# Seven block products for a third of K in h · w_out of a fused float64 attention and MLP kernel

## The chip, the cores and the metric

The kernel runs on one core of a Trainium2 chip. The metric is device time in microseconds (us) of the slowest core (here the only one); lower is better. Times of the kernel before and of the changed one are medians of several runs; the profile is one more execution, with a time of its own.

## The reference, cut to what matters

Three blocks follow one another. Window attention gives 2304 tokens of 512 columns, `x`. Then two gated networks, all in matrix products:

```python
g, val = x @ w_gate, x @ w_val            # 512 -> 1536
h = g * sigmoid(g) * val                  # 2304 x 1536
x2 = h @ w_out                            # 1536 -> 512, the product that the change touches
a, b = x2 @ w1, x2 @ w2                   # 512 -> 1024
out = ((a * b) @ w3) @ w_out2             # done as (a * b) @ (w3 @ w_out2)
```

## The kernel before, in words

**Words and passes.** Weights arrive as 64-bit numbers and are narrowed to 32 bits by VectorE (DVE) and ScalarE (ACT). Each 32-bit operand is split into two words, a high one (a `cast`, on ACT) and what is left (a `rest`, on DVE). A product of two blocks is three passes over the words: high x high, high x low, low x high (`PASSES`). A matmul works on 128 x 128 weights and 384 token columns (`T`).

**The stages.** First the attention (to about 113 us). The second stage (`gated`, to 363 us) computes h; the third (`project`, to 513 us) computes x2; the fourth (`gated` again, to 688 us) computes a * b; then `final` multiplies w3 by w_out2 and the result by that. Tokens are worked in three groups of 768 (`tp`), each as two halves of 384.

**Seven products in `gated`.** A unit is one pair of 128-column blocks of one weight for one token group. Its 2 x 2 block product is done with seven products of six matmuls (numbers 1 to 7, list `PRODUCTS`) instead of eight. Product 1 goes into a PSUM bank `al`; ACT copies it (negated) out into a tile `c11`; product 2 goes into a bank `ga` of its own, and DVE adds it to `c11` (L699). Products 6, 7 and 4 add onto `al`, with a copy by ACT (L377) after each of the first two; products 5 and 3 share a bank `be`. ACT then applies the Silu (L712) or DVE multiplies the two halves of the gate (L709). `AT` says in which slot of the order a product stands; a unit starts every seven slots, so that two units interleave. The finished h goes to DRAM (`store`, L777).

**The third stage in `project`, plain.** For each token group eight banks `acc[m, x]` collect 12 row blocks `f` of w_out's K: in each, 4 column blocks m, 2 token halves x, 3 passes, so 24 matmuls (L852), 288 in a group. Row tiles of h (`Rows`: 128 x 768, two row blocks, one token half) come from DRAM (`pl`, on SP's queue), get their high word on ACT (`ph`, L218) and their rest on DVE (L227). 16 tiles of w_out's words stay resident through all three groups. At a group's end ACT (L835, and the negated ones L377) and DVE (L838) evict the eight banks into `X2`. `Operands` then makes the fourth stage's operands from it: 14 casts, 14 rests and 8 sums for each group.

**w_out's words.** `Split.make` narrows a 256-row piece of w_out, splits it in two steps of 512 columns (L218, L227) and stores it to DRAM, from where `Resident.queue` loads it. It is interleaved with the gate weights in the list `coming`, through two staging buffers (`st`), so that a load waits until the piece two before it is made.

**What sets the order.** All engines' instructions are put in line by hand under `manual_schedule`. `Plan` keeps a model clock for each engine; small work (splits, loads, DMAs) is queued as a `Job` with a cost, a rank and a due time, and `fill` places what is ready between the products. `need` places a job at once when a product asks for it. `slots` counts free tiles of the pool `sl`. Each engine, and each DMA queue (SP's, and POOL's for adding DMAs), then works strictly in the order in which it was given its instructions. `events1` and `events_p` tie queueing of loads to units and row blocks. Lines named by the trace: L687 a product's matmul in `gated`, L852 in `project`, L377 a copy by ACT, L699 an add by DVE, L811 the load of a row tile, L263 the load of a staging buffer.

## Time and profile before

| what | us |
|---|---|
| runs: median (lowest to highest), 3 runs | 823.98 (823.34 to 825.07) |
| the profiled execution, its own time | 825.91 |
| its span, first to last instruction | 824.2 |
| PE busy in the span | 815.6 |
| third stage, `project` | 150.0 |

PE is TensorE's matmuls, PEld its weight loads, SPq and POOLq the DMA queues of SyncE and GpSimd. Times in rows are us from the span's start unless they say ns. In a row of groups the name `out<-in` is what is written and read, with buffer numbers left out, `x` and a number is how many instructions, then busy us, mean ns of one, and the idle time before them with what ended it. Matmuls are pipelined, so a matmul lasts 334 ns while the next starts 173 ns after it.

### The profile page before, as it was taken

How to read it: one execution, taken by the hardware profiler on the slowest of the kernel's cores; microseconds unless marked ns; L12 is line 12 of the kernel's file. 1: busy time of each engine (PE TensorE's matmuls, PEld its weight loads, DVE VectorE, ACT ScalarE, POOL GpSimd, SP SyncE). 2: the span in 40 equal slices, each digit the busy share in tenths (PEclk: the TensorE clock that was granted, in tenths of full speed). 3: DMA queues.
4: the chain of work that ended last, by engine and by line, in shares of the span. 5: the costliest groups of instructions: out<-in, count | busy, mean ns of one | idle time of the engine just before them, and what ended most of it. 6: DMA issues, size and time to landing. Idle time of an engine off the chain costs nothing.

```text
span 824.2 us, 15599 instructions
## 1 busy us (share of the span) xinstructions
PE 815.6 (99%) x5718; PEld 785.2 (95%) x5718; DVE 640.6 (78%) x1354; ACT 454.6 (55%) x1194; POOL 92.4 (11%) x135
## 2 busy tenths in 40 slices
PE   9999999999999999999999999999999999999998
PEld 6777899999999999999999999999999998899997
DVE  5999889686887939865888683877888844789994
ACT  7899987555555535633564551444444423755543
POOL 3666833000000000000000000000010100000000
PEclk9999999999999999999999999999999999999999
DMA  9989396253562344599996722024555289007632
GB/s 187 199 186 199 61 217 125 90 192 128 192 229 83 137 153 161 210 360 380 385 290 157 233 71 103 20 83 142 167 180 175 110 299 335 27 2 207 181 73 78
DMA packets 172766, 140.23 MB, mean 170 GB/s; under 512 B 120849, under 2 KB 142609, under 8 KB 171665
## 3 DMA queue, kind: packets, MB, share of 16 engines
q1 hardware_dynamic: 167888, 125.86, 50.8%
q0 software_dynamic: 4800, 13.37, 5.9%
q8 instruction: 45, 0.74, 0.4%
...
## 4 chain that ended last, share of the span: by engine, by line
PE 90%; SPq 4%; DMA 2%; ACT 1%; DVE 1%; issue 1%; ACTq 0%
PE o L852 18%; PE ala L687 15%; PE alb L687 14%; PE bea L687 7%; PE beb L687 7%; PE acc L1010 5%; PE al L1153 4%; PE gaa L687 4%; PE gab L687 3%; SPq L403 2%; PE be L1153 2%; PE al L1085 2%; PE PV L519 2%; PE PT L499 2%; PE S L466 1%; PE T L429 1%
## 5 line engine op out<-in xcount | busy, mean ns | idle before, releaser
L852 PE MATMUL o<-ph,wo 128*128 128x384 f32 x576 | 146.4, 334 | 0.0
L852 PEld LDWEIGHTS o<-ph,wo 128*128 128x128 f32 x576 | 104.1, 188 | 0.0
L852 PE MATMUL o<-pl,wo 128*128 128x384 f32 x288 | 96.3, 334 | 0.0
L377 ACT ACTIVATE ha<-ala 128x384 f32<-128x384 f32 x102 | 49.6, 488 | 50.0 <-PE ala L687 49.3
L777 POOL DMA_DIRECT2D h<-ha x24 | 13.0, 546 | 548.2 <-DVE ha L709 548.2
L699 DVE TENSOR_TENSOR ha<-ha,bea 128x384 f32<-128x384 f32 x60 | 33.2, 553 | 38.3 <-PE bea L687 22.3
L852 PEld LDWEIGHTS o<-pl,wo 128*128 128x128 f32 x288 | 54.1, 188 | 0.3 <-DVE pl L227 0.3
L480 ACT ACTIVATE pexp<-S,stat 128x128 f32<-128x128 f32 x144 | 53.1, 421 | 0.0
L218 ACT CAST hf<-h 128x384 fp32r<-128x384 f32 x84 | 38.8, 513 | 14.5 <-DVE h L231 13.2
L712 ACT ACTIVATE ha<-ha 128x384 f32<-128x384 f32 x54 | 28.4, 526 | 33.1 <-DVE ha L699 33.1
L227 DVE TENSOR_TENSOR hf<-h,hf 128x384 fp32r<-128x384 f32 x84 | 42.3, 548 | 4.8 <-ACT hf L218 4.8
L227 DVE TENSOR_TENSOR pl<-pl,ph 128x768 fp32r<-128x768 f32 x36 | 33.4, 953 | 14.6 <-ACT ph L218 14.3
L218 ACT CAST ph<-pl 128x768 fp32r<-128x768 f32 x36 | 29.1, 839 | 26.2 <-DMA pl<-h 23.6
L490 POOL TENSOR_TENSOR pexp<-pexp,stat 128x384 f32<-128x384 f32 x48 | 39.1, 835 | 28.6 <-DVE stat L487 14.1
L377 ACT ACTIVATE c12b<-alb 128x384 f32<-128x384 f32 x30 | 14.8, 492 | 48.7 <-PE alb L687 48.6
L480 ACT ACTIVATION_READ_ACCUMULATOR pexp<-S,stat 128x1 f32 x144 | 37.2, 260 | 0.0
L699 DVE TENSOR_TENSOR c22b<-c22b,beb 128x384 f32<-128x384 f32 x30 | 16.6, 553 | 25.8 <-ACT c22b L377 25.8
L687 PE MATMUL ala<-xo,w_g_7h 128*128 128x384 f32 x120 | 30.4, 336 | 0.5 <-ACT ha L377 0.5
L687 PE MATMUL ala<-xo,w_g_1h 128*128 128x384 f32 x126 | 29.2, 335 | 0.0
L473 DVE TENSOR_REDUCE stat<-S 128x3 f32<-128x384 f32 x48 | 24.4, 550 | 4.8 <-PE S L466 4.4
L218 ACT CAST xp<-X 128x384 fp32r<-128x384 f32 x42 | 19.7, 520 | 10.5 <-DVE X L231 7.5
L377 ACT ACTIVATE c11b<-alb 128x384 f32<-128x384 f32 x30 | 14.7, 490 | 19.2 <-PE alb L687 19.2
...
## 6 DMA issues: line engine op xcount, KB each, us to landing
...
```

Of the source, the lines that this page charges most:

```text
L218: (eng.copy if eng is nc.scalar else eng.tensor_copy)(out=hi(), in_=src())
L227: return plan.job(lambda eng: eng.tensor_tensor(out=lo(), in0=src(), in1=hi().bitcast(F32), op=ALU.subtract), after, slots=slots, due=due, ...
L377: nc.scalar.mul(out=out, in_=in_, mul=-1.0)
L473: nc.vector.tensor_reduce(out=st[:, 0, x, :], in_=sc[2 * m + x], op=ALU.max, axis=AX.X, negate=True)
L480: nc.scalar.activation(out=pe[:, jj, :], in_=so[:, jj, :], func=AF.Exp, bias=st[:, 0, x, jj:jj + 1], accum_out=st[:, 1, x, jj:jj + 1])
L490: nc.gpsimd.tensor_tensor(out=pe, in0=pe, in1=st[:, 3, x, :].unsqueeze(2).to_broadcast([P, SUB, P]), op=ALU.mult)
L687: nc.tensor.matmul(acc, lhsT=self.wt.ops[p, x][:, m, :], rhs=self.xs.ops[p, m][:, y, :], start=start and n == 0, stop=n == 5, skip_group_c ...
L699: nc.vector.tensor_tensor(out=out, in0=x, in1=y, op=ALU.add)
L712: nc.scalar.activation(out=h, in_=src, func=func, scale=-1.0 if direct else 1.0)
L852: nc.tensor.matmul(acc[m, x], lhsT=wos.tiles[i // 6][:, i % 6, :], rhs=rows[2 * tp + x].words(f, b), start=f == n == 0, stop=f == NF - 1 a ...
L1010: nc.tensor.matmul(acc, lhsT=w3T[i][c // 3][:, x, (c % 3) * P:(c % 3) * P + P], rhs=zt[c, y], start=c == k == 0, stop=c == NI - 1 and k == 2)
L1153: nc.tensor.matmul(acc, lhsT=right.ops[p, m, y][:, P * k:P * k + P], rhs=self.xs.ops[p, m][:, x, :], start=bool(name) and n == 0, stop=n = ...
```

## The change

It does the first two of the six 256-row pairs of w_out's K (`SEVEN`) as seven products per token group, the other four (`plain`) block by block as before. In `project` product 1 goes into a bank `al`, ACT copies it into a second bank (`seed`), and product 2 and later the plain blocks are added there by TensorE; product 7 seeds a fourth bank in the same way. The sums of h's blocks that the seven products need are made in DRAM: the second stage writes h's blocks of the first two pairs several times (`spread`), with the sign of the diagonal ones turned in the last multiplication, and POOL's queue issues four adding DMAs for each token group as soon as the second pair is stored. A new class `Seven` makes w_out's words for the seven products, with four sums for each piece. Units from number 6 on, counted from 0 (`SEEDED`), in both `gated` stages use the same seeding for product 2 and do product 5 ahead of it (`AT_SEEDED`). w_out's words are queued directly behind the weight ahead of them in the list, with a due time, and at the weights' rank. Row tiles have a budget of their own (8 loaded, 6 high words) and are loaded strictly in turn; resident tiles of w_out become 20. The last pair's units stand in another order (`ENDS`). The fourth stage's operands of the first two token groups wait for a mark that the third group's second step sets (`opened`).

```diff
 AT = {1: 0, 2: 2, 5: 3, 6: 4, 7: 8, 4: 12, 3: 13}
...
+AT_SEEDED = {1: 0, 5: 2, 2: 3, 6: 4, 7: 8, 4: 12, 3: 13}
...
-    NSLOT = 56
+    NSLOT = 58
...
-    half = ctx.enter_context(tc.tile_pool(name="half", bufs=7))
+    half = ctx.enter_context(tc.tile_pool(name="half", bufs=5))
...
+            if j.large:
+                j.done = self.landed = max(j.done, self.landed + 2.6)
+            if j.rows:
+                self.rows[j.rows] -= 1
...
-                        if j.slots and self.slots < j.slots + self.keep:
+                        if j.slots and self.slots < j.slots + self.keep or j.rows and (self.rows[j.rows] < 1 or j.behind and j.behind.done is None):
...
+    SEEDED = 6
+    SEVEN = (0, 1)
+    stored = {}
...
-                if self.x and direct:
+                if self.x and (direct or i == t and func != AF.Copy and self.fp in SEVEN):
                     nc.vector.scalar_tensor_tensor(out=h, in0=src, scalar=-1.0, in1=h, op0=ALU.mult, op1=ALU.mult)
                     plan.charge("DVE", dve(T))
...
+                elif (i, t) == (0, 0) and self.seeded:
+                    nc.scalar.copy(out=h, in_=src)
+                    plan.charge("ACT", act(T))
...
-                    self.c11 = self.own(0, 0, "c11")
+                    self.seeded = self.n >= SEEDED
+                    if self.seeded:
+                        self.ga = bank(f"ga{self.name}")[:, :T]
+                    self.c11 = self.ga if self.seeded else self.own(0, 0, "c11")
                     later(1, lambda: self.copy(self.c11, self.al))
+                elif p == 2 and self.seeded:
+                    plan.wait(self.read)
+                    self.mm(self.ga, 2)
+                    self.put(0, 0, self.ga)
                 elif p == 2:
-                    ga = bank(f"ga{self.name}")[:, :T]
-                    self.mm(ga, 2, True)
-                    self.add(self.c11, self.c11, ga)
+                    self.ga = bank(f"ga{self.name}")[:, :T]
+                    self.mm(self.ga, 2, True)
+                    self.add(self.c11, self.c11, self.ga)
...
-                        for i, t in enumerate(hs.pop((self.fp, self.tp))):
-                            store(out=hd[self.fp, self.tp][:, i, :], in_=t)
-                        plan.slots += 2
+                        h = hs.pop((self.fp, self.tp))
+                        if func != AF.Copy and self.fp in SEVEN:
+                            spread(self.fp, self.tp, h)
+                        else:
+                            for i, t in enumerate(h):
+                                store(out=hd[self.fp, self.tp][:, i, :], in_=t)
+                            plan.slots += 2
+                            done = mark()
+                            done.done = plan.charge("DVE", 0.0) + 4.0
+                            stored[self.fp, self.tp] = [done]
...
-        when = [(7 * n + AT[p], n, p) for n in range(len(units)) for p in PRODUCTS if (n, p) != (len(units) - 1, 2)]
+        when = [(7 * n + (AT_SEEDED if n >= SEEDED else AT)[p], n, p) for n in range(len(units)) for p in PRODUCTS if (n, p) != (len(units) - 1, 2)]
...
+    H_AT = {1: 0, 7: 1, 2: 2, 3: 3, 4: 4, 6: 5, 5: 6}
+    def spread(fp, tp, h):
+        to, f = h7d[tp], SEVEN.index(fp)
+        (h0, h1) = (t.rearrange("p (c t) -> p c t", c=2) for t in h)
+        for at, src in (((0, 2), h0), ((2, 4), h1), ((4, 6), h1), ((6, 7), h0[:, :1])):
+            nc.sync.dma_start(out=to[:, at[0]:at[1], f, :], in_=src)
+        plan.slots += 2
+        if fp == SEVEN[1]:
+            keep, plan.rank = plan.rank, SPREAD_RANK
+            done = mark()
+            done.done = plan.charge("DVE", 0.0) + 5.0
+            def add(p, by, after):
+                j = plan.job(lambda eng: eng.dma_start(out=to[:, H_AT[p]], in_=to[:, H_AT[by]], accum_op=ALU.add),
+                             [done, *after], lag=8.0, DMA=1.0)
+                stored[p, tp, 7] = [j]
+                return j
+            s5 = add(5, 7, [])
+            add(7, 3, [s5])
+            s6 = add(6, 5, [s5])
+            add(4, 6, [s6])
+            for p in (1, 2, 3):
+                stored[p, tp, 7] = [done]
+            plan.rank = keep
...
+        before = None, None
+        def __init__(self, tp):
+            self.tp = tp
...
+                eng.dma_start(out=self.lo[key].bitcast(F32),
+                              in_=h7d[self.tp][:, H_AT[f]] if x == 7 else h1d[f, self.tp][:, :, T * x:T * x + T])
...
+            a = loading(load, stored[key[0], self.tp, 7] if key[1] == 7 else stored[key[0], self.tp], rows=1, lag=9.0, due=due)
+            b = cast(hi, lambda: self.lo[key].bitcast(F32), [a], 2 * T, 0, rows=2, due=due)
+            (a.behind, b.behind), Rows.before = Rows.before, (a, b)
+            self.jobs[key] = rest(lambda: self.lo[key], lambda: self.lo[key].bitcast(F32), lambda: self.hi[key], [b], 2 * T, due=due)
+        def words(self, key, g, x):
+            return (self.lo if x else self.hi)[key][:, g, :]
+    STEPS = (1, 5, 6, 2, 7, 3, 4)
...
-            acc = {(m, x): bank(f"o{tp}_{m}_{x}")[:, :T] for m in range(NM) for x in range(2)}
...
-            for f in range(NF):
...
-                            plan.need(wos.jobs[i // 6])
-                            nc.tensor.matmul(acc[m, x], lhsT=wos.tiles[i // 6][:, i % 6, :],
-                                             rhs=rows[2 * tp + x].words(f, b),
-                                             start=f == n == 0, stop=f == NF - 1 and n == 2)
...
-            if tp == NTP - 1:
-                for m, x in acc:
-                    evict(m, x)
-            xop2[tp] = Operands([lambda x=x: x for x in x2], f"xp{tp}")
...
+            al, ga, be, de = ([None] * 2 for _ in range(4))
...
+            def seed(to, src, m, name):
+                open_bank(to, m, name)
+                nc.scalar.copy(out=to[m], in_=src[m])
+                plan.charge("ACT", act(T))
...
+            def copy(r, c, src, m):
+                (negated if r == c else nc.scalar.copy)(out=part(r, c, m), in_=src[m])
+                plan.charge("ACT", act(T))
+            def add(r, c, src, op, m):
+                nc.vector.tensor_tensor(out=part(r, c, m), in0=part(r, c, m), in1=src[m], op=op)
+                plan.charge("DVE", dve(T))
+            def product(acc, key, w, g, m, start=False, stop=False):
+                plan.need(r.jobs[key])
+                for n, (x, y) in enumerate(PASSES):
+                    plan.need(wos.job(w, g, x, m))
+                    nc.tensor.matmul(acc, lhsT=wos.words(w, g, x, m), rhs=r.words(key, g, y),
+                                     start=start and n == 0, stop=stop and n == 2, skip_group_check=not start)
...
+            for k, p in enumerate(STEPS):
+                for event in events.get((tp, k), ()):
                     event()
...
+                to = {2: ga, 5: be, 3: be}.get(p, al)
+                for m in range(2):
+                    if p in (1, 5):
+                        open_bank(to, m, "al" if p == 1 else "be")
+                    for g in range(2):
+                        product(to[m], (p, 7), p, g, m, p in (1, 5) and g == 0, True)
+                    if p == 1:
+                        seed(ga, al, m, "ga")
+                    elif p == 5:
+                        copy(1, 1, be, m)
+                    elif p == 6:
+                        copy(0, 1, al, m)
+                    elif p == 7:
+                        seed(de, al, m, "de")
+                    if m:
+                        freed(1)
+                        if tp == NTP - 1:
+                            wos.used(k)
+                    plan.advance(PRODUCT)
+                    yield
+            for k, fp in enumerate(plain):
+                for event in events.get((tp, len(STEPS) + k), ()):
+                    event()
+                for g in range(2):
+                    last = g == 1 and fp == plain[-1]
+                    for b, (i, c, to) in enumerate(((1, 0, al), (0, 1, be), (0, 0, ga), (1, 1, de))):
+                        for m in range(2):
+                            product(to[m], (fp, c), (fp, i), g, m, False, last)
+                            if last:
+                                if (i, c) == (1, 0):
+                                    copy(1, 0, al, m)
+                                elif (i, c) == (0, 1):
+                                    add(0, 1, be, ALU.add, m)
+                                elif (i, c) == (0, 0):
+                                    copy(0, 0, ga, m)
+                                else:
+                                    add(1, 1, de, ALU.subtract, m)
+                        if b == 1 or b == 3:
+                            if b == 3 and g:
+                                freed(2)
+                                if tp == NTP - 1:
+                                    wos.used(len(STEPS) + 2 * k)
+                                    wos.used(len(STEPS) + 2 * k + 1)
+                            plan.advance(2 * PRODUCT)
+                            yield
+            xop2[tp] = Operands([lambda x=x: x for x in x2], f"xp{tp}", dict.fromkeys(PRODUCTS, opened), X2_SUMS, X2_RESTS, due=14.0 * tp)
...
+    class Seven(Doubles):
+        GROUPS = ((1, 2), (5, 6), (7, 3), (4,))
...
+                for q, p in enumerate(group):
+                    after, due = list(ready), self.due + k + q
+                    if p in sums:
+                        x, y, op = sums[p]
+                        after = after + [made.get({6: 5, 3: 6}.get(p))]
...
+                        made[p], after = j, [j]
...
+                    a = cast(hi, lambda p=p: self.words(*at[p]), after + by[-2:-1], n, 0, p == 1, due=due)
+                    b = rest(lambda p=p: ops[p][:, 1], lambda p=p: self.words(*at[p]), lambda p=p: ops[p][:, 0], [a], n, 0, p == 1, due)
+                    self.last += [a, b]
+                    jobs.append(b)
+                def put(eng, group=group, t=t):
+                    for q, p in enumerate(group):
+                        eng.dma_start(out=w7d[p][:, SEVEN.index(self.n)], in_=t[0][:, q].rearrange("p x f -> p (x f)").bitcast(F32))
+                by.append(plan.job(put, jobs, lag=5.0, SP=0.5 * len(group)))
+                for p in group:
+                    self.stored[p] = by[-1]
...
+    h7d = [dram.tile([P, 7, 2, T], F32, name=f"h7_{tp}") for tp in range(NTP)]
+    w7d = {p: dram.tile([P, 2, 512], F32, name=f"w7_{p}") for p in STEPS}
...
-    wo = [Split(w_out, n, "wo", put_wo) for n in range(NF2)]
+    wo = [Seven(w_out, n) if n in SEVEN else Split(w_out, n, "wo", put_wo) for n in range(NF2)]
...
-            plan.rank = rank if rank is not None else 1 if isinstance(coming[at[1]], Weights) else 2
+            plan.rank = rank if rank is not None else 2 if coming[at[1]] in w3s else 1
...
             plan.rank = 0
+        if at[1] < len(coming) and (coming[at[1]] in wo or isinstance(coming[at[1]], Plain)):
+            coming[at[1]].due = coming[at[1] - 1].due + 7.0
+            make_to(coming[at[1]], rank, ahead)
...
-    passed = {(tp, f): mark() for tp in range(NTP) for f in range(DF // P)}
...
+        def queue(self, k, due):
+            for s in range(4 * k // 3, -(-4 * (k + 1) // 3)):
+                if s in self.jobs:
+                    continue
+                parts = sorted({768 * s // 1024, (768 * s + 767) // 1024})
...
+                after = []
+                for q in parts:
+                    f, x = self.sources[q]
+                    after += [wo[fp].stored[f] for fp in SEVEN] if x == 7 else [wo[f // 2].stored[f % 2]]
+                self.jobs[s] = plan.job(load, after, lag=7.0, slots=1, due=due, SP=0.5 * len(parts))
...
+    def project_loads(tp):
...
+        for k, p in enumerate(STEPS):
+            rows[tp].queue((p, 7), 100 * tp + k)
+        for k, fp in enumerate([fp for fp in range(NF2) if fp not in SEVEN]):
             for x in range(2):
...
+                rows[tp].queue((fp, x), 100 * tp + len(STEPS) + 2 * k + x)
...
-    order1 = unit_order(NF2, [(x, tp) for x in range(2) for tp in range(NTP)])
-    order2 = unit_order(NI2, [(0, 0), (0, 1), (1, 0), (1, 1), (0, 2), (1, 2)])
+    ENDS = [(0, 0), (0, 1), (1, 0), (1, 1), (0, 2), (1, 2)]
+    order1, order2 = unit_order(NF2, ENDS), unit_order(NI2, ENDS)
...
-    on(events1, last1 - 2, lambda: make_to(wo[-1]))
-    on(events1, last1 - 1, lambda: project_loads(0, range(1)))
-    on(events1, last1, lambda: project_loads(0, range(1, NF2)))
+    ROWS = (8, 6)
+    def share():
+        plan.slots -= sum(ROWS)
+        plan.rows[1:] = ROWS
+    on(events1, last1 - 2, lambda: (make_to(wo[-1]), weight_loads(0, 4)))
+    on(events1, last1 - 1, lambda: (share(), project_loads(0), weight_loads(4, 7)))
+    on(events1, last1, lambda: weight_loads(7, 9))
     events_p = {}
-    on(events_p, (0, 0), lambda: (setattr(plan, "landing", 10.0), make_to(w3s[NW3 - 1])))
+    on(events_p, (0, 0), lambda: (setattr(plan, "landing", 10.0), setattr(plan, "keep", 0), make_to(w3s[NW3 - 1])))
+    for n in range(3):
+        on(events_p, (0, 2 * n), lambda n=n: weight_loads(9 + 2 * n, 11 + 2 * n))
+    on(events_p, (0, 7), lambda: project_loads(1))
+    on(events_p, (1, 7), lambda: project_loads(2))
+    opened = mark()
+    X2_SUMS, X2_RESTS = (), ()
+    SPREAD_RANK = 0
+    on(events_p, (1, 4), lambda: make_to(left2[0, 1], 0))
+    on(events_p, (2, 1), lambda: reach(opened))
     on(events_p, (2, 0), lambda: setattr(plan, "landing", 6.0))
-    on(events_p, (1, 6), lambda: make_to(left2[0, 1], 0))
-    on(events_p, (0, 6), lambda: project_loads(1, range(NF2)))
-    on(events_p, (1, 6), lambda: project_loads(2, range(NF2)))
...
+        plan.slots += sum(ROWS)
+        plan.keep = 3
+        on(events2, 6, lambda: setattr(plan, "keep", 2))
```

## Rows read from the trace of the kernel before

**Rows 1.** The page, busy time of each engine (part 1).
```profile
PE 815.6 (99%) x5718; PEld 785.2 (95%) x5718; DVE 640.6 (78%) x1354; ACT 454.6 (55%) x1194; POOL 92.4 (11%) x135
```

**Rows 2.** The chain that ended last: start us, us, what.
```profile
363.35 149.99 PE o L852 x864
```

**Rows 3.** Waits of PE, whole span: us in total, times, longest us.
```profile
PE alb L687 <- ACT c22b L377: 0.8, 1, 0.8
PE ala L687 <- ACT ha L377: 0.5, 1, 0.5
```

**Rows 4.** Windows: us, then PE, PEld, DVE, ACT, POOL busy (instructions), PEclk, DMA share, GB/s.
```profile
113.65:363.35 249.70, 248.90 (x1431) 248.03 (x1432) 195.56 (x411) 140.42 (x310) 10.13 (x12) 1.00 0.51 168
363.35:378.00 14.65, 14.65 (x87) 14.65 (x86) 11.07 (x19) 6.51 (x9) 0.00 (x0) 1.00 1.04 379
378.00:413.35 35.35, 35.35 (x205) 35.08 (x204) 23.07 (x36) 16.09 (x25) 0.00 (x0) 1.00 1.02 385
413.35:513.35 100.00, 100.00 (x578) 100.00 (x578) 72.45 (x134) 46.01 (x86) 0.00 (x0) 1.00 0.57 171
513.35:530.00 16.65, 16.65 (x98) 16.65 (x97) 12.42 (x27) 8.86 (x20) 0.00 (x0) 1.00 0.00 1
530.00:688.07 158.07, 158.07 (x913) 158.07 (x913) 120.25 (x252) 67.72 (x150) 11.92 (x22) 1.00 0.54 168
```

**Rows 5.** Groups by line, DVE and ACT in the third stage (363.35 to 513.35).
```profile
L227 DVE TENSOR_TENSOR pl<-pl,ph 128x768 fp32r<-128x768 f32 x34 | 31.6, 953 | 14.6 <-ACT ph L218 14.3
L227 DVE TENSOR_TENSOR xp<-X,xp 128x384 fp32r<-128x384 f32 x28 | 14.4, 549 | 0.0
L838 DVE TENSOR_SCALAR X<-o 128x384 f32<-128x384 f32 x8 | 4.5, 558 | 19.0 <-PE o L852 19.0
L218 ACT CAST ph<-pl 128x768 fp32r<-128x768 f32 x34 | 27.6, 840 | 26.2 <-DMA pl<-h 23.6 <-PE o L852 2.3
L835 ACT COPY X<-o 128x384 f32<-128x384 f32 x8 | 3.8, 491 | 22.4 <-PE o L852 22.4
```

**Rows 6.** Groups by line, DVE and ACT in the second stage (113.65 to 363.35).
```profile
L699 DVE TENSOR_TENSOR c11b<-c11b,gab 128x384 f32<-128x384 f32 x17 | 9.3, 547 | 0.0
L227 DVE TENSOR_TENSOR by_wo<-st_wo,by_wo 128x512 fp32r<-128x512 f32 x12 | 8.1, 690 | 2.8 <-ACT by_wo L218 2.4
L231 DVE TENSOR_TENSOR st_v<-st_v 128x256 f32<-128x256 f32 x20 | 7.8, 419 | 0.0
L377 ACT ACTIVATE c11b<-alb 128x384 f32<-128x384 f32 x17 | 8.3, 487 | 4.3 <-PE alb L687 4.3
L218 ACT CAST by_wo<-st_wo 128x512 fp32r<-128x512 f32 x12 | 7.7, 654 | 0.0
L218 ACT CAST w_v_1h<-st_v 128x256 fp32r<-128x256 f32 x11 | 4.2, 412 | 0.0
```

**Rows 7.** Timeline, 298.83 to 311.54: start us, us, engine, what, [idle before].
```profile
298.83 0.43 SPq L263 DMA_DIRECT2D st_g<-in_moe_w_gate_dram  x1
308.31 0.77 DVE L194 TENSOR_SCALAR st_g<-st_g 128x512 int32<-128x512 int32 x2 [2.77 <-DMA st_g<-in_moe_w_gate_dram]
308.69 0.33 PE L687 MATMUL alb<-xo,w_v_1l 128*128 128x384 f32 x1
311.54 0.49 ACT L377 ACTIVATE c11b<-alb 128x384 f32<-128x384 f32 x1
```

**Rows 8.** Waits of ACT in the third stage.
```profile
ACT ph L218 <- DMA pl<-h: 23.6, 10, 6.6
```

**Rows 9.** The tile pl: its loads, and who waited for them.
```profile
  DVE pl L227: 0.3, 1
DMA to landing us min/median/max: 3.5/6.1/9.2
```

**Rows 10.** DMA issues: KB each, median us to landing.
```profile
X<-X POOLq DMA_DIRECT2D x10, 192.0 KB, 5.5
```

156 lines of the change are left out of this document (84 added, 72 removed).

## The prediction

> **What bounds the kernel now.** I read the page's busy times first, for the engine with the least room: TensorE (PE) is busy for 815.6 of 824.2 us, VectorE (DVE) for 78%, ScalarE (ACT) for 55% [rows 1]. Then the chain that ended last, to see whether the stage that the change cuts lies on it: the whole third stage, h times w_out, is one piece of 149.99 us with 864 matmuls and nothing in between [rows 2]. That is 149.99 / 864 = 0.1736 us a matmul, and 6 x 0.1736 = 1.04 us for a product of six. So a matmul less in this stage shortens the program, as long as nothing else becomes late. Then the waits of PE, to see what there is to win beside that: the two named in the second stage are 0.8 and 0.5 us [rows 3]; nothing in the third stage is long enough to be listed. Last the windows by stage: PE is full at granted clock 1.00 from 363 to 688 us, while DVE has 106.6 of 150 us (11.07 + 23.07 + 72.45) and ACT 68.6 in the third stage, and the DMA engines are full from 363 to 413 us, at 379 and 385 GB/s [rows 4]. PE sets the time; DVE, ACT and DMA have room on average, but DMA has none where the third stage starts.
>
> **What the change takes off PE.** For each of the three token groups the four row blocks of K that come from h's first two column pairs cost 4 x 4 x 2 x 3 = 96 matmuls before. As seven products of 2 x 2 x 3 they cost 84. The other eight row blocks keep their 192. So 3 x 12 = 36 matmuls go, at the pace of [rows 2]: 36 x 0.1736 = **6.25 us**. The copies that seed a bank are ACT's, so PE gets nothing new.
>
> **What it adds in the third stage.** Nine row tiles more (45 for 36): each costs one cast of 0.840 us on ACT and one rest of 0.953 us on DVE [rows 5], so 7.6 and 8.6 us. Twelve seeds and eight ACT evictions more (24 for 16) at 0.491 us add 9.8 us to ACT; twelve DVE adds stand for eight DVE evictions of 0.558 us, 2 us more. DVE then has about 106.6 + 8.6 + 2 = 117 of 144 us, ACT 86 of 144. Both stay below PE, so as work this costs nothing. If that cover is gone (an engine that stands in front of a wait), the price is a wait of PE, below.
>
> The seeds are a new wait for PE. Product 6 adds onto the bank whose copy seeded another, and starts four blocks after product 1's first block: 4 x 1.04 = 4.16 us, less 1.20 until that block's last matmul ends, less 0.49 for the copy, leaves 2.47 us in which ACT may be late. Product 7's seed and product 4 stand in the same distance. Behind the copy on ACT stand the casts of later row tiles; in front of it may stand a cast whose tile has not landed.
>
> **What it changes in the second stage.** The words of the two w_out pairs: per pair 4 sums and 7 rests of 256 columns at about 0.42 us for 2 rests of 0.690 us on DVE, so +3.2 us; 7 casts of 0.412 us for 2 of 0.654 on ACT, +1.6 us [rows 6]. Twice that is 6.5 and 3.3 us. Against it 30 of 36 units lose an add of 0.547 us (16.4 us). DVE gets 10 us of room in 250. In the fourth stage 18 units lose the add (9.8 us) and nine ACT copies come (4.4 us) beside 67.7 us in 158 [rows 4]: free too.
>
> A seeded unit puts product 5 ahead of product 2, and product 2 now waits for ACT's copy of product 1 into its bank. From the start of product 1 that is 3 x 1.04 = 3.12 us, less 1.20, less 0.487 [rows 6]: 1.43 us of slack. Nothing in the rows copies into a PSUM bank; the nearest is this copy out of one, 0.487 us, and I take it. (The Trainium skill, ScalarE: Activation LUTs, section "Step-by-step: what each stage is for", calls a ScalarE result into PSUM the lower-latency one; by it the slack would be a little larger; no row here shows it.) In the timeline one unit would have missed the slack: its first product ended at 309.02 us and the copy started at 311.54, 2.5 us later, 1.1 over the slack, in the stretch where DVE stood 2.77 us for a weight tile whose load was issued at 298.83 [rows 7]. That same stretch holds the 0.8 us wait of [rows 3]. The change makes w_out's words in line by due times, so the staging buffer comes free earlier and this load with it: between 0 and 0.8 us won, or 1.1 lost if the load stays late. I take **-0.4** for the load and **+0.2** for the tighter wait (bounds 0 and 48 x 0.1 = 4.8, taken near zero because only this one stretch exceeds the slack).
>
> **Row tiles, loads, adds in DRAM.** The longest ACT wait for a row tile is 6.6 us, ten waits make 23.6 [rows 8]; PE's weight loads stood only 0.3 us for a row tile, once, with tile loads that take 3.5 to 9.2 us to land [rows 9]. After the change a step of 2.08 us eats one row tile where 8.3 us ate two, but eight tiles and nine weight sources are queued before the stage begins. Bounds 0 and the rivals' prices; I take **+0.2**, the size of the one loss seen. The twelve adds in DRAM move 384 KB each; an adding DMA of 192 KB lands in 5.5 us [rows 10], so I estimate 11 us each and 44 for the chain of four; they are issued when the second pair's last unit ends, 24 of 36 units (24 x 7.28 = 175 us) before the first use. POOL's queue holds nothing else then, so a wait there delays nobody. The spread stores (24 issues for 12 on SP) lie behind the same last DVE product as the two stores did and ahead of loads due units later: nothing. The smaller pool of half tiles: the units need two where they needed three: nothing. Four more resident tiles and their issues go on SP with the other loads, from three units before the stage instead of two: no cost beyond rival (a). The last pair's units in another order free two groups' operands a unit earlier, which is what gives those loads their slots. The words of the fourth stage's first two weights move some 17 us earlier in the second group (step 4 at 8.3 us for row block 6 at 25 us): the same DVE and ACT work, in a window where DVE has 72.45 of 100 us [rows 4], behind the row tiles by rank; nothing.
>
> **The sum.** -6.25 - 0.4 + 0.2 + 0.2 = -6.25 us. Against the profiled execution's own 825.91 us (824.2 of span and 1.7 around it) that is 819.7; the median of the runs, 823.98, is 1.9 us below that execution, so the forecast is **817.7**, with 816.2 to 819.2 as its own range.
>
> **Rivals.** (a) *The start of the third stage runs short of bytes.* Seven steps eat 7 x 384 KB of rows and 7 x 512 KB of weights, 6.42 MB in 7 x 2.08 = 14.6 us: 440 GB/s, where the rows show 379 with the engines full [rows 4]. At that rate they take 16.9 us, 2.3 us more; with one cast 6.6 us late and 2.47 of slack it is 4.1. About 3.4 us lost: 821.1. For it: share 1.04 there already. Against: most of it is queued in the last two units, and those loads stand ahead in SP's order. By the Trainium skill (Perfetto Trace Analysis, section Roofline) a core's 16 DMA engines bound it at about 435 GB/s; by that figure, an estimate, the same bytes take 14.8 us and this price all but vanishes; no row here exceeds 385.
>
> (b) *Slower: ACT's order becomes PE's.* In all three groups a cast that waits for its tile stands in front of a seed. At 6.6 us [rows 8] less 2.47 each costs 4.1 us, three times 12.4: 830.1. It decides for slower from two such waits on (8.2 us). For it: ten such waits exist. Against: the rows of the steps are queued a stage ahead, and in the later groups DMA falls to 171 GB/s.
>
> (c) *The fourth stage starts short of operands.* Two groups' operand words are held back to the third group's second step: 2 x (14 rests + 8 sums) x 0.549 = 24.2 us on DVE, beside 15 x 0.953 + 4 x 0.55 = 16.5, so 40.7 of 46 us. If the second group's 12.1 us slip past the stage, DVE's free quarter there (12.42 busy of 16.65) gives 3.7 us before unit 2 and 3.4 within it: 5.0 us lost, 822.7. Against: the first group, needed at once, is made first.
>
> **How the numbers follow.** A measurement of this kernel tells 0.2%, 1.65 us, from no change. Forecast 0.60, (a) 0.17, both faster; (c) 0.09, no difference; (b) 0.14, slower. So faster 0.77, same 0.09, slower 0.14. For 8 in 10 the range takes the forecast, (a) and (c): 816.0 to 823.2.
>
> **What would show it.** 828 matmuls in the third stage in about 143.7 us, in one piece on the chain; no PE wait over 0.3 us on ACT's seeds; the 0.8 us wait at 314 gone; DVE near 117 us there. Wrong: PE waits on a row tile or weight tile in the first 15 us of the stage (a), on a seed behind a cast in each group (b), or on operand words in the first two units of the fourth stage (c).

## The result, and the profile after

| | us |
|---|---|
| changed kernel, median (lowest to highest), 4 runs | 832.26 (832.11 to 834.19) |
| before, on the same chip, 4 runs | 824.06 (823.34 to 825.07) |
| ratio, 95% interval | 1.0103 [1.0084, 1.0121] |
| span of the profiled execution (its own time 832.3) | 830.5, before 824.2 |

The kernel is 1.0% slower; 817.7 was forecast, with a range of 816.0 to 823.2. TensorE's busy time on the page hardly falls, though it has 36 matmuls less (compare [rows 1]):

```profile
PE 814.4 (98%) x5682; PEld 781.7 (94%) x5682; DVE 631.2 (76%) x1337; ACT 476.3 (57%) x1242; POOL 102.9 (12%) x147
```

The windows by stage of the changed kernel (columns as in [rows 4]) show where the time went:

```profile
113.65:371.25 257.60, 251.11 (x1425) 248.06 (x1424) 186.94 (x399) 145.94 (x322) 19.00 (x22) 0.99 0.67 214
371.25:421.50 50.25, 48.12 (x276) 47.48 (x275) 36.46 (x58) 25.09 (x40) 0.00 (x0) 1.00 1.01 376
421.50:471.20 49.70, 49.70 (x277) 49.70 (x278) 36.84 (x58) 25.49 (x43) 0.00 (x0) 0.97 0.93 273
471.20:519.00 47.80, 47.80 (x278) 47.80 (x277) 38.87 (x78) 28.91 (x61) 0.00 (x0) 1.00 0.28 92
519.00:535.00 16.00, 16.00 (x94) 15.99 (x93) 14.30 (x31) 9.68 (x22) 0.00 (x0) 1.00 0.17 67
535.00:694.00 159.00, 158.85 (x916) 158.53 (x916) 112.83 (x239) 72.20 (x160) 12.15 (x22) 1.00 0.54 168
```

The second stage takes 257.60 us where it took 249.70 [rows 4]: 7.9 us lost. Of the third stage's three token groups the last runs as forecast, 47.80 us (276 matmuls at the old pace are 276 x 0.1736 = 47.9, before it was 50.0). The first two take 50.25 and 49.70, 4.2 us more than that together. So the stage as a whole is 147.75 us for 149.99, not 143.7. The fourth stage takes 16.0 + 159.0 us for the 16.65 + 158.07 of [rows 4], the same within 0.3 us. Next, PE's waits from 113.65 to 530 us (total, times, longest; [rows 3] answer to them):

```profile
PE beb L699 <- DVE c22b L711: 2.2, 1, 2.2
PE al L922 <- ACT X L911: 1.9, 1, 1.9
PE gaa L699 <- ACT gaa L385: 1.9, 3, 1.1
PE alb L699 <- ACT c22b L385: 1.1, 1, 1.1
PE beb L699 <- DVE w_v_5l L234: 0.7, 1, 0.7
PE beb L699 <- ACT w_v_4h L225: 0.5, 1, 0.5
```

The 0.8 us wait of [rows 3] at 314 us is gone, as forecast; these are others. The largest is the one that ends at 221.4 us. VectorE's timeline and PE's there:

```profile
219.56 0.77 DVE L201 TENSOR_SCALAR st_g<-st_g 128x512 int32<-128x512 int32 x2 [5.93 <-DMA st_g<-in_moe_w_gate_dram]
220.25 0.67 DVE L204 SCALAR_TENSOR_TENSOR st_g<-st_g 128x512 int32<-128x512 int32 x1
220.84 0.54 DVE L711 TENSOR_TENSOR c22b<-c22b,beb 128x384 f32<-128x384 f32 x1
```

```profile
221.44 1.86 PE L699 MATMUL beb<-xo,w_v_3h 128*128 128x384 f32 x5 [2.16 <-DVE c22b L711]
```

VectorE stood 5.93 us for the staging buffer `st_g` to land; the add of `c22b`, which TensorE needed, was queued behind it and started only at 220.84. Why the buffer was late, the DMA view of 180 to 240 us tells, first of the changed kernel, then of before:

```profile
q1 hardware_dynamic: 5236, 10.55, 47.5%
q0 software_dynamic: 1728, 4.72, 44.5%
...
h<-h POOLq DMA_DIRECT2D x12, 384.0 KB, 10.2
...
st_wo<-in_moe_w_out_dram SPq DMA_DIRECT2D x2, 1024.0 KB, 13.7
...
st_g<-in_moe_w_gate_dram SPq DMA_DIRECT2D x1, 1024.0 KB, 11.7
```

```profile
st_wo<-in_moe_w_out_dram SPq DMA_DIRECT2D x2, 1024.0 KB, 6.3
st_g<-in_moe_w_gate_dram SPq DMA_DIRECT2D x1, 1024.0 KB, 5.5
```

The queue q0 does not exist in this stretch before. It holds the twelve adding DMAs, and they take 44.5% of all sixteen engines for 60 us: 26.7 us, **2.2 us of the whole DMA system for each 384 KB**. The loads beside them land after 13.7 and 11.7 us, where they took 6.3 and 5.5.

The other wait of about 2 us, which ends at 421.5 us, is at the boundary of the third stage's first two groups. ScalarE's timeline there:

```profile
415.83 0.65 ACT L225 CAST by_z<-st_z 128x512 fp32r<-128x512 f32 x1 [1.90 <-DMA zd<-by_z]
416.39 1.57 ACT L225 CAST ph<-pl 128x768 fp32r<-128x768 f32 x2
420.39 0.70 ACT L210 ACTIVATE st_w<-st_w 128x512 f32<-128x512 f32 x1 [2.43 <-DVE st_w L204]
420.98 0.85 ACT L911 COPY X<-al 128x384 f32<-128x384 f32 x2
```

ScalarE stands 1.90 us until a store of z's words has landed, casts two row tiles, stands 2.43 us for VectorE, and only then makes the eviction (L911) that frees TensorE's bank.

### The profile page after: what moved, and what is told of

Read it like the earlier page. It is cut to its first block, busy times and chain, and to the rows that moved or that the text cites. A ratio compares the mean times of both kernels' runs of the same rounds, so it can differ in the third digit from the quotient of the medians.

```text
span 830.5 us, 15689 instructions
## 1 busy us (share of the span) xinstructions
PE 814.4 (98%) x5682; PEld 781.7 (94%) x5682; DVE 631.2 (76%) x1337; ACT 476.3 (57%) x1242; POOL 102.9 (12%) x147
## 4 chain that ended last, share of the span: by engine, by line
PE 78%; DMA 9%; SPq 4%; DVE 4%; ACT 3%; issue 1%; ACTq 0%
PE alb L699 12%; PE ala L699 12%; PE beb L699 6%; PE bea L699 6%; PE acc L1119 5%; PE al L922 5%; PE al L1262 4%; PE be L922 4%; DMA st_wo<-in_moe_w_out_dram 3%; PE gab L699 3%; PE gaa L699 3%; PE ga L922 3%; SPq L411 2%; PE be L1262 2%; PE de L922 2%; PE al L1194 2%
## 5 line engine op out<-in xcount | busy, mean ns | idle before, releaser
L922 PE MATMUL al<-ph,wo 128*128 128x384 f32 x192 | 54.7, 338 | 1.9 <-ACT X L911 1.9
L385 ACT ACTIVATE ha<-ala 128x384 f32<-128x384 f32 x78 | 38.2, 490 | 26.1 <-PE ala L699 26.0
L234 DVE TENSOR_TENSOR pl<-pl,ph 128x768 fp32r<-128x768 f32 x45 | 41.9, 950 | 12.6 <-ACT ph L225 12.2
L922 PE MATMUL be<-ph,wo 128*128 128x384 f32 x144 | 42.1, 340 | 0.0
L922 PEld LDWEIGHTS al<-ph,wo 128*128 128x128 f32 x192 | 35.4, 189 | 2.2 <-ACT X L911 2.2
L724 ACT ACTIVATE ha<-ha 128x384 f32<-128x384 f32 x39 | 20.5, 526 | 25.0 <-DVE ha L711 25.0
L922 PE MATMUL ga<-ph,wo 128*128 128x384 f32 x120 | 34.8, 334 | 0.0
L922 PE MATMUL al<-pl,wo 128*128 128x384 f32 x96 | 32.3, 337 | 0.0
L922 PE MATMUL de<-ph,wo 128*128 128x384 f32 x96 | 28.2, 334 | 0.0
L718 DVE SCALAR_TENSOR_TENSOR ha<-alb,ha 128x384 f32<-128x384 f32 x30 | 16.6, 553 | 15.0 <-PE alb L699 14.8
```

The source lines that it names most:

```text
L234: return plan.job(lambda eng: eng.tensor_tensor(out=lo(), in0=src(), in1=hi().bitcast(F32), op=ALU.subtract), after, slots=slots, due=due, ...
L385: nc.scalar.mul(out=out, in_=in_, mul=-1.0)
L724: nc.scalar.activation(out=h, in_=src, func=func, scale=-1.0 if direct else 1.0)
L922: nc.tensor.matmul(acc, lhsT=wos.words(w, g, x, m), rhs=r.words(key, g, y), start=start and n == 0, stop=stop and n == 2, skip_group_check ...
```

## The experiments

The numbers are the order of the runs; where two belong together they stand together. Microseconds after "Measured" are medians. The runs were made on several chips, so kernels are compared by their ratios: each is to the kernel before, run on the same chip, with its 95% interval. I held three theories at first. A: the adding DMAs' use of the engines. B: w_out's words made in line. C: the seeds, which make TensorE wait for ScalarE in each unit.

**1. The adds gone.** In `spread`:

```diff
-                j = plan.job(lambda eng: eng.dma_start(out=to[:, H_AT[p]], in_=to[:, H_AT[by]], accum_op=ALU.add),
-                             [done, *after], lag=8.0, DMA=1.0)
-                stored[p, tp, 7] = [j]
-                return j
+                stored[p, tp, 7] = [done]
+                return done
```

> The changed kernel without its twelve adding DMAs in DRAM (the row tiles of products 5, 7, 6 and 4 then hold unsummed blocks of h; everything else is done). Theory A, the adds fill the DMA engines between 186 and 233 us of the changed kernel, so that staged weights land in 11.7 and 13.7 us where 6 was planned, and DVE, which stands in front of them, makes PE wait: the waits at 200, 219 and 234 us go with the low clock behind the second, 0.5 + 4.2 + 1.4 = 6 us, so about 826. Theory B, w_out's words in line are what stands in front of PE's work: the waits stay, 832. Theory C, the seeds' tighter wait: it stays within 1 us of 832.

Measured: 826.15 us, ratio 1.0016 [0.9996, 1.0036], span 824.0. The window of the bad stretch (columns as above), first of the changed kernel, then of run 1:

```profile
180.00:240.00 60.00, 56.45 (x314) 55.49 (x313) 43.13 (x98) 30.68 (x69) 10.21 (x12) 0.97 0.92 256
180.00:240.00 60.00, 60.00 (x348) 60.00 (x347) 47.44 (x105) 33.02 (x73) 0.00 (x0) 1.00 0.58 208
```

TensorE is full where it had stood for 3.5 us; counted in matmuls, it had done 34 fewer in these 60 us, 5.9 us of work at 0.1736 each, as part of the others ran at a lower clock (last section). None of its waits from 180 to 250 us is left, and `st_wo` and `st_g` land after 6.3 and 7.2 us. So about 0.87% of the 1.03% goes with the adds (1.0103 - 1.0016), some 7 us: theory A's number. The adds did it through the loads and not by slowing VectorE: for instance, its sums of `st_g`'s blocks (128x256) take 417 ns beside the adds and 418 without them. But the kernel without its sums is only level with before: there is a second loss, near the gain's size.

**2. One add a unit.** Each add waits, in the planner, for a mark that units 14 to 25 set.

```diff
-                             [done, *after], lag=8.0, DMA=1.0)
+                             [done, next(turn), *after], lag=8.0, DMA=1.0)
...
+    for i, m in enumerate(turns):
+        on(events1, 14 + i, lambda m=m: reach(m))
```

> The changed kernel with the twelve adds held back and let go one at a time, at the start of units 14 to 25. Theory A: the same 6 us less, about 826, since one add alone leaves the DMA engines room. If the adds cost by their bytes wherever they stand, the waits only move to later units: 830 to 833. Theories B and C: 832.

Measured: 830.21, 1.0058 [1.0029, 1.0087]. Theory A's 826 is missed; 830 to 833 was forecast if the bytes cost the same wherever they stand. What the edit really did is told with run 5.

**3. w_out's words not in line.** `make_to` as it was before, with its ranks.

```diff
-            plan.rank = rank if rank is not None else 2 if coming[at[1]] in w3s else 1
+            plan.rank = rank if rank is not None else 1 if isinstance(coming[at[1]], Weights) else 2
...
-        if at[1] < len(coming) and (coming[at[1]] in wo or isinstance(coming[at[1]], Plain)):
-            coming[at[1]].due = coming[at[1] - 1].due + 7.0
-            make_to(coming[at[1]], rank, ahead)
```

> The changed kernel with w_out's words (and w3's) made as in the kernel before: at the lower rank, when the next weight is asked for. Theory B: the waits at 200, 234 and 337 us go, 0.5 + 1.4 + 1.7 = 3.6 us, so about 828.5. Theory A: the loads that land late are late all the same, the 4.2 us at 219 stay; 831 to 834, slower where a weight waits for its staging buffer again.

Measured: 844.3, 1.022 [1.0175, 1.0264]. The longest wait of PE:

```profile
PE ala L699 <- ACT ha L385: 5.0, 1, 5.0
```

The two waits on w_v's words (0.7 and 0.5 us) do go, but larger ones come, and the change loses another 1.2% (1.022 - 1.0103), some 10 us. Making the words in line does not cost what theory B thought: it fell.

**4. No seeds in units.**

```diff
-    NSLOT = 58
+    NSLOT = 57
...
-    half = ctx.enter_context(tc.tile_pool(name="half", bufs=5))
+    half = ctx.enter_context(tc.tile_pool(name="half", bufs=7))
...
-    SEEDED = 6
+    SEEDED = 99
```

> The changed kernel with no seeded units (product 2 into a bank of its own and a DVE add, product 2 ahead of product 5, as before), with 7 half tiles and one slot less for the room they need. Theory C: the three waits of product 2 on the seeding copy go, 0.5 + 1.4 + 0.7 = 2.6 us, so about 829.5. Theory A: those three waits are only where a late DVE or ACT first shows; without them the same lateness meets product 6 one slot later, so 831 to 833, and the wait at 219 us stays.

Measured: 863.54, 1.0472 [1.0428, 1.0515]. PE's longest wait is 5.0 us for a word of w_v. The run is confounded: VectorE gets its adds back and the pool loses a slot. It shows only that the seeds are no loss to be had back by undoing them; theory C fell in that form.

**5 to 7. The adds at quiet units, then two repairs of order.** The marks of run 2 at units 16 to 30 (5); besides, `coming` with w_v's piece 5 ahead of w_out's piece 4 (6); besides, z's store reckoned at 8 us (7):

```diff
+    for n, m in zip((16, 17, 19, 21, 22, 22, 25, 25, 27, 28, 30, 30), turns):
+        on(events1, n, lambda m=m: reach(m))
...
+    coming.remove(wo[4])
+    coming.insert(coming.index(wo[5]), wo[4])
...
-                by.append(plan.job(lambda eng, j=j, t=t: self.put(eng, 2 * self.n + j, t[0]), [b], lag=5.0, SP=0.5))
+                by.append(plan.job(lambda eng, j=j, t=t: self.put(eng, 2 * self.n + j, t[0]), [b], lag=8.0 if self in z else 5.0, SP=0.5))
```

> The changed kernel with its twelve adding DMAs let go one or two at the start of units 16, 17, 19, 21, 22, 22, 25, 25, 27, 28, 30, 30 of the second stage instead of all together behind the stores; nothing else differs, so the same bytes are moved. Theory A (the adds are dear because twelve of them, about 2.2 us of all sixteen DMA engines each, stand ahead of st_g and st_wo between 195 and 235 us): the staging loads of 190 to 240 us land after 9 us or less, the waits at 200, 219 and 234 us go, and the time is 825 to 827, like the kernel without the adds. Rival (the bytes cost the same wherever they are moved, since the stage's DMA share is 0.67 throughout): loads land late at other places instead and the time is 829 to 832.

> As the kernel with the adds in quiet units, and the words of w_v's piece 5 are made before those of w_out's piece 4 (the change's new order of units uses piece 5 one unit sooner). If the wait of 1.6 to 2 us near 332 to 337 us is only this order, it goes and the time falls by 1 to 2 us, to about 824.5. Rival (VectorE has too much to do there, whichever piece comes first): the wait moves to w_out's piece 4 or to c22b's copies and the time stays within 0.5 us of the kernel before it in this list.

> As the kernel with piece 5 first, and the planner reckons 8 us instead of 5 for the landing of z's stored words, so that ScalarE's cast behind such a landing is placed later. If ScalarE's standing on that DMA (1.9 us at 418 us) is what makes TensorE wait at the boundary of the third stage's first two groups, that wait of about 2 us goes, and with it the matmuls at half pace that follow it: 822 to 823.5. Rival (ScalarE has as much to do there anyhow): another tile's cast or eviction ends the wait and the time stays within 0.7 us.

Measured: 830.18, 1.0079 [1.0047, 1.011]; 833.39, 1.0096 [1.0062, 1.013]; 831.39, 1.009 [1.0059, 1.012]. Theory A's number seems missed in run 5. But POOL's timeline of that run shows that the edit did not do what it said:

```profile
183.38 0.86 POOL L851 DMA_DIRECT2D h<-h  x1 [53.15 <-DMA h<-ha]
...
241.38 0.81 POOL L851 DMA_DIRECT2D h<-h  x1 [7.83 <-DMA h<-h]
```

The adds go out from 183 to 241 us, as in run 2 (in the changed kernel from 183 to 227). A mark of the planner delays only the place in the program; POOL's queue holds nothing else and waits for nothing but the data, so it runs ahead of the units. Runs 2 and 5 are misses as tests of place. Runs 6 and 7 did what they should to their own waits (none near 335 us in either, none at the group boundaries in run 7), but a new one of 4.7 and 4.2 us appeared after 380 us, on the cast of a row tile; neither is faster than run 5, and both forecasts were missed.

**8. The adds in the kernel before.** Its h is also stored spread, into a tile that nothing reads, and added there:

```diff
+                        if func != AF.Copy and self.fp < 2:
+                            spread(self.fp, self.tp, h)
...
```

> The kernel before, with h's two row tiles also stored spread into a DRAM tile that nothing reads, and the twelve adding DMAs on it in second-stage order as the change has them; the products, the words and the seeds are those of before. It stores 4.8 MB more than the change (8.3 MB more than before, where the change stores 3.5 MB more), all within the second stage. Theory A (the adds by themselves, by their use of the DMA engines, cost what was lost): waits for staging loads come at 200 to 240 us in this kernel too and the time is 827 to 832. Rival (the adds hurt only because the change's words in line and seeds leave no slack): 825 or less.

**12. The same without the adds.**

> The kernel before with the same extra spread stores (8.3 MB more, nothing reads them) as the one with stores and adds, and without the twelve adds. It splits that kernel's loss of 18.6 us: if the adds carry it, this one is within 2 us of before (824 to 826); if the stores' bytes do, it is at 835 to 842; equal shares would be 831 to 835.

Measured: 842.48, 1.0227 [1.0191, 1.0263] with stores and adds; 827.33, 1.0045 [1.0026, 1.0065] with the stores alone. The stores cost 3.7 us, the twelve adds the other 1.8%, 15 us, in a kernel with none of the change's other parts. Run 8's longest wait of PE (there are 4.8 MB more of stores around the adds than in the change):

```profile
PE ala L687 <- ACT ha L377: 10.1, 3, 7.4
```

The load of `st_g` between 180 and 240 us, in run 8 and in run 12:

```profile
st_g<-in_moe_w_gate_dram SPq DMA_DIRECT2D x1, 1024.0 KB, 13.2
```

```profile
st_g<-in_moe_w_gate_dram SPq DMA_DIRECT2D x1, 1024.0 KB, 5.6
```

Theory A's mechanism stands without the rest of the change; its number (827 to 832) is missed: here the adds cost 15 us instead of 7. Why twice as much, no run shows.

**9. The sums on GpSimd in SBUF,** in place, each stored once:

```diff
+        for at, y, x in ((6, h0[:, 0, :], h0[:, 1, :]), (1, h0[:, 1, :], h1[:, 1, :]), (5, h1[:, 1, :], h0[:, 0, :]), (4, h1[:, 0, :], h1[:, 1, :])):
+            nc.gpsimd.tensor_tensor(out=y, in0=y, in1=x, op=ALU.add)
+            nc.gpsimd.dma_start(out=to[:, at, f, :], in_=y)
...
```

> The changed kernel with h's four sums made in SBUF by four GpSimd additions for each finished pair of h's row tiles (24 in all), and each sum stored once; the twelve adding DMAs are gone, everything else is as in the change, and the output is whole. Theory A (what the adding DMAs take of the sixteen engines is the loss): the staging loads of 190 to 240 us land as in the kernel without adds, the waits at 200, 219 and 234 us are gone, and the time is 825 to 827, equal to before within 0.3%. Rival (the sums themselves come too late for the row tiles however they are made, or GpSimd's additions slow VectorE beside them): TensorE waits for row tiles near 375 us or for VectorE's copies between 180 and 240 us and the time is 829 or more.

**11. The same with z's store reckoned at 8 us.**

> The kernel with GpSimd's sums, and 8 us instead of 5 reckoned for the landing of z's stored words. If the wait at the boundary of the third stage's first two groups (1.5 to 2 us at 414 us) and that at the next (0.8 to 2 us at 468 us) are ScalarE standing on that landing, both go and the time is 1.5 to 3 us under that of the kernel before it in this list, about 823. Rival (the planner's other choices shift with it and a row tile comes late near 380 us, as in the run with piece 5 first): a wait of 4 to 5 us near 380 us, and 826 to 829.

Measured: 847.39, 1.0271 [1.0236, 1.0307]; 841.79, 1.0216 [1.0168, 1.0264]. The rival held, in its second half. (4.8 us of run 9 are another thing: X's DMAs of 129 us stood behind the sums in GpSimd's queue.) VectorE's groups from 180 to 220 us, in run 9 and, the same lines and tiles, in run 1 (columns as in [rows 5]):

```profile
L718 DVE SCALAR_TENSOR_TENSOR ha<-c22b,ha 128x384 f32<-128x384 f32 x3 | 3.7, 1218 | 0.1
L238 DVE TENSOR_TENSOR st_g<-st_g 128x256 f32<-128x256 f32 x4 | 3.5, 897 | 0.0
...
L718 DVE SCALAR_TENSOR_TENSOR ha<-alb,ha 128x384 f32<-128x384 f32 x3 | 1.6, 548 | 0.0
```

```profile
L718 DVE SCALAR_TENSOR_TENSOR ha<-alb,ha 128x384 f32<-128x384 f32 x3 | 1.7, 550 | 0.0
L238 DVE TENSOR_TENSOR st_g<-st_g 128x256 f32<-128x256 f32 x4 | 1.6, 416 | 0.0
...
L718 DVE SCALAR_TENSOR_TENSOR ha<-c22b,ha 128x384 f32<-128x384 f32 x2 | 1.1, 558 | 0.1
```

Two groups with both inputs in SBUF last twice as long on average in the stretch in which GpSimd adds: 1218 for 558 ns (`c22b`) and 897 for 416. The first one's line with one input in a PSUM bank (`alb`) does not: 548 for 550. The Trainium skill (SBUF — State Buffer, section "Who interferes with whom") states that a VectorE instruction with two inputs in SBUF contends with a GpSimd instruction that reads SBUF, as they share a port; the row of `st_g` (two inputs in SBUF) is such an instruction and agrees, 897 for 416 ns. Some with a single input in SBUF were slower too: line L201 (`st_v`, 128x512) took 1470 ns in run 9 and 422 in run 1. In run 11 the waits at the group boundaries were gone, so the lag works, but under losses of this size the time says little.

**10. The adds held back in fact,** each behind a one-column GpSimd copy that reads what its unit has just computed:

```diff
+                    if func != AF.Copy and self.n in let_go:
+                        nc.gpsimd.tensor_copy(out=held_by, in_=hs[self.fp, self.tp][0][:, :1])
+                        for m in let_go[self.n]:
+                            reach(m)
...
```

> The changed kernel with its twelve adding DMAs held, each by a one-column GpSimd copy that reads what product 2 of its unit has just given: units 16, 17, 19, 21, 22, 22, 25, 25, 27, 28, 30, 30 (in the earlier two kernels meant to spread them, only the planner's mark was moved and GpSimd's queue let them go between 183 and 241 us all the same). They now issue from about 230 to 332 us, where the DMA share of the kernel without adds is 0.44 to 0.67 instead of 0.58 with the stores. Theory A in its strict form (engine time is dear only where the queues are full): waits at 200, 219 and 234 us go, nothing comes in their place, 825 to 827. Rival (each add delays the load behind it wherever it is, as TensorE's operands have little slack in every unit): waits of 0.5 to 2 us come between 240 and 340 us, and the time is 828 to 832.

Measured: 828.05, 1.0045 [1.0023, 1.0066]. POOL's timeline, the DMA view of 240 to 340 us, and two windows:

```profile
219.05 0.86 POOL L856 DMA_DIRECT2D h<-h  x1 [0.24 <-DMA st_wo<-in_moe_w_out_dram]
...
331.97 0.81 POOL L856 DMA_DIRECT2D h<-h  x1 [4.22 <-DMA h<-h]
```

```profile
q0 software_dynamic: 1440, 3.93, 27.2%
...
h<-h POOLq DMA_DIRECT2D x10, 384.0 KB, 4.8
```

```profile
180.00:240.00 60.00, 60.00 (x348) 60.00 (x347) 47.63 (x106) 32.98 (x73) 2.72 (x5) 1.00 0.67 222
240.00:300.00 60.00, 58.31 (x334) 57.35 (x333) 42.30 (x91) 33.83 (x76) 5.86 (x9) 1.00 0.68 194
```

Now they go out from 219 to 332 us, each lands after 4.8 us instead of 10.2, and TensorE is full from 180 to 240 us. But ten of them still take 27.2% of 100 us, 2.7 us each. TensorE stands 1.7 us from 240 to 300 instead (0.5 in run 1), in waits of up to 0.9 us. Place is worth about 0.6% (1.0103 - 1.0045), 4.8 us of the 7; what is left to run 1, 0.29% or 2.4 us, the adds cost wherever they are. Theory A in its strict form is missed; the rival has the kind of wait and, at its lowest end, the number.

**13 to 16. The second loss.** The adds held (13, 14) or gone (15, 16), each with piece 5 first and the lag of 8 us; in 14 and 15 z's further loads are queued six steps later:

```diff
-    on(events_p, (0, 0), lambda: (setattr(plan, "landing", 10.0), setattr(plan, "keep", 0), make_to(w3s[NW3 - 1])))
+    on(events_p, (0, 0), lambda: (setattr(plan, "landing", 10.0), setattr(plan, "keep", 0)))
+    on(events_p, (0, 6), lambda: make_to(w3s[NW3 - 1]))
```

> Adds held by units as before, with w_v's piece 5 made first and 8 us reckoned for z's stored words. If the waits named (about 2 us at 335, 1 to 2 at 418 and 471 us) are independent of the row tiles, all go and the time is 824 to 825. If the third stage's start is short of bytes, TensorE only gets there sooner and waits 4 to 5 us for a row tile's cast near 380 us: 827 to 830.

> The same, with the queueing of z's remaining loads put off from the first step of the third stage to its seventh (about 10 us), so that up to two loads of 1 MB leave the stretch of 358 to 400 us (a full load takes about 2.6 us of all engines at the 400 GB/s seen there). If bytes make the wait at 380 us, it falls by 2.5 to 5 us and the time is 822 to 824.5. Rival (the row tile is late by the order of SyncE's queue or by its slots, not by bytes): the wait stays and the time is within 1 us of the kernel before it in this list.

> Without the adding DMAs (the row tiles of products 5, 7, 6 and 4 hold h's blocks unsummed), with piece 5 first, the lag of 8 us and z put off: what the change could give if its sums cost nothing. If all the named waits are accounted for, 819 to 821 (before less 6.25 us of TensorE and plus at most 3 us of small waits); if something else takes the gain, 823 or more.

> The same without z put off. By the account with bytes the wait at 380 us is here as in the kernels with adds (4 to 5 us), and the time is 823 to 825; by the account with the adds' traffic (their last add lands at 337 us and pushes loads into the third stage) there is no such wait and the time is 819 to 821.5.

Measured: 828.83, 1.0068 [1.0051, 1.0085]; 829.22, 1.0066 [1.0049, 1.0082]; 827.29, 1.0048 [1.0033, 1.0063]; 827.04, 1.0043 [1.0028, 1.0059]. All four have the wait after 380 us (4.1 to 4.7 us), with adds and without, with z's load and without; so neither makes it. In run 13:

```profile
PE be L930 <- ACT ph L225: 4.1, 1, 4.1
```

```profile
357.00 1.30 SPq L1411 DMA_DIRECT2D wo<-by_wo  x2
...
361.90 4.76 SPq L1497 DMA_DIRECT2D wo<-w  x5
...
377.14 0.56 SPq L883 DMA_DIRECT2D pl<-h  x1
```

With piece 5 first, the words of w_out's piece 4 are made later and stored at 357 us (L1411). The third stage's weights follow in SyncE's queue, and the row tile that TensorE needs at 380 is issued behind them, at 377.14. My repair of one wait had made this one. The wait also cost more than its length: the next 4 us ran at a granted clock of 0.50, the lower level, and the third stage took 150.7 to 151.9 us in these four runs.

**17 and 18. Piece 5 asked for one unit sooner, the order left alone,** and the lag of 8 us; adds held (17) and gone (18):

```diff
-                    on(events, n if fp else 3, lambda l=left, f=fp + x, y=1 - x: make_to(l[f, y]))
+                    on(events, n - (left is left1 and (fp, x) == (NF2 - 1, 0)) if fp else 3, lambda l=left, f=fp + x, y=1 - x: make_to(l[f, y]))
```

> Adds held by units; w_v's piece 5 is asked for one unit sooner (the order of the pieces is the change's); 8 us reckoned for z's stored words. If the waits at 336 us (about 2 us) and at 418 and 471 us (about 1.5 us together) were late words and ScalarE's standing, and w_out's piece 4 is stored in time, they go, no wait comes at 380 us, and the time is 824 to 825.5. Rival (every microsecond that the second stage gains is lost again at 380 us, since all sixteen engines are full from 358 us on): a wait of 2 to 5 us at 380 us and 827 to 829.

> The same without the adding DMAs (products 5, 7, 6 and 4 get h's blocks unsummed). By the first account 821 to 823.5, under before for the first time; by the rival 825.5 to 827, like the three other kernels without adds.

Measured: 826.16, 1.0037 [1.0024, 1.0049]; **822.44, 0.9983 [0.997, 0.9996]**. Three of run 18's waits, and the issue of the row tile:

```profile
PE alb L699 <- ACT c22b L385: 1.2, 1, 1.2
...
PE beb L699 <- DVE w_v_5l L234: 0.7, 1, 0.7
PE be L920 <- DVE pl L234: 0.6, 1, 0.6
```

```profile
372.23 3.04 SPq L873 DMA_DIRECT2D pl<-h  x2
```

The waits at the group boundaries and the 4 us wait after 380 are gone in both. In run 18 TensorE comes to the third stage about as early as in the four runs before (first matmul at 364.6 us; there 363.1 to 365.1), and the DMA engines are as full from 358 to 385 us (share 1.03; 1.04 in run 13). So that wait was the order of SyncE's queue, not bytes alone. (Run 17 comes there only at 368.6 us and can't tell the two accounts apart.) The third stage takes 144.2 us in run 17 and 144.5 in run 18, where 143.7 was forecast. Asking sooner did not cure the wait on piece 5 (0.7 us still); the first account held for the lag and for the order, while run 17's time is above its range of 824 to 825.5.

Run 18 leaves h's sums out and is the only one under before, by 0.17%, 1.4 us. Run 17, the best that makes the whole product, is 0.37% over before. The sums cost 1.0037 - 0.9983 = 0.54% between these two, **4.4 us even when held apart**, most of the 6.25 us that the products save. In the other pairs the price of held adds is smaller: 0.29% (runs 10 and 1), 0.25% (13 and 16) and 0.18% (14 and 15), 1.5 to 2.4 us; there the two intervals overlap, and other waits follow, which may hide a part.

## Why the prediction was wrong

- **Failed step: the adds in DRAM, costed at nothing** because they are issued "24 of 36 units (24 x 7.28 = 175 us) before the first use" and "POOL's queue holds nothing else then, so a wait there delays nobody". The step priced their latency and their own queue, not the sixteen engines that they share with every load. DRAM to DRAM with an addition, 4.72 MB took 26.7 us of the engines, 177 GB/s, where the queue of plain transfers beside it moved 10.55 MB in 47.5% of 60 us, 370 GB/s. The 60 us had a DMA share of 0.58 without them (run 1) and 0.92 with them. They cost about 7 us as the change issues them, and 1.5 to 4.4 us when held apart. The row that I used, the landing time of one adding DMA [rows 10], says nothing of this. The trace of before had the price: from 95 to 125 us, where GpSimd's queue holds adding DMAs alone,

```profile
q0 software_dynamic: 1813, 2.49, 50.2%
```

which is 2.49 MB in 15.1 us of the engines, 165 GB/s. By that the twelve adds come to 4.72 / 165 = 28.6 us, near the 26.7 measured.
- **The saving** of 6.25 us was right: 47.80 us in the undisturbed group against 47.9 reckoned. VectorE was busy for 112.2 us of the stage (117 reckoned) and ScalarE for 79.5 (86); as work neither set the time.
- **The load of the staging buffer, -0.4.** The wait at 314 us went, but the last pair's other order uses w_v's piece 5 a unit sooner, and 0.7 and 0.5 us came at 338 to 340 us, and 1.1 on `c22b` at 369, behind the casts of queued row tiles. I had looked at what that order frees, not at what it needs earlier. The sum without adds is therefore not -6.25 but, in run 18, -1.4 us (0.9983). Its profile tells where most of that went: the third stage is 5.5 us shorter than before (144.5 for 150.0), but the second, with waits of 2.9 us for 1.0, is 2.6 us longer (252.6 for 250.0, counted over its last 1431 matmuls). That makes -2.9; the 1.5 us between it and the medians stay open.
- **The tighter wait of seeded units, +0.2:** 1.9 us in three waits, right in kind; with the adds gone 0.5. The 0.1 us a unit in its upper bound stands in no row. The slack was reckoned with a copy of 0.487 us; in the changed kernel from 113 to 530 us the copies from a bank into a bank (`gaa<-ala`, 15 of them) take 475 ns, those from a bank into SBUF (`c22b<-alb`, 18) 488, so 13 ns less. The Trainium skill (ScalarE: Activation LUTs, section "Step-by-step: what each stage is for") calls PSUM the lower-latency port; the trace agrees in sign, but 13 ns decide nothing here.
- **Words made in the third stage.** The prediction costs the fourth stage's first weights there at nothing, "behind the row tiles by rank", and does not price z's (the words of w_out2). ScalarE's program is in fixed order, and a cast of z that waits for a store to land holds the eviction behind it: 1.9 us, and 1.2 more at the lower clock that followed. With 8 us reckoned instead of 5 no wait of PE on ScalarE at a group boundary is left in any of the eight kernels with that edit (runs 7, 11 and 13 to 18); without it runs 1, 2, 3, 5, 6, 9 and 10 have one or two each, of 0.3 to 1.9 us.
- **The spread stores costed at nothing.** Run 12 puts 8.3 MB of such stores into the kernel before and loses 0.45%, 3.7 us; the change stores 3.5 MB more than before. What these alone cost in it no run shows.
- **Rival (a)**, short of bytes at the start of the third stage: not in the changed kernel (its wait there is 0.2 us, for a rest). The wait it names did come after 380 us in six of the experiments (6, 7, 13 to 16), but by the order of the queue.
- **Rival (b)** gave 830.1, close to the measured time, by luck: it wanted ScalarE in front of a seed in all three groups. One boundary on an eviction is what came, and the larger part of the loss is in the second stage, where it had nothing. A wait on a seed does stand in some experiments without the longer lag (0.6 us in run 1, 1.6 in run 5), once in each.
- **Rival (c)** did not come: VectorE has 14.30 of 16.00 us busy at the start of the fourth stage, but PE's only wait for an operand word in that stage is 0.15 us, at 554 us, and the stage runs as before.

What stays open: whether VectorE could make the sums; in run 1 it has 60.00 - 47.44 = 12.6 us free in the window of 180 to 240 us. That was not tried.
